# Four gate/up phases in a row, then four down phases, in a gated mix of linear attention and a GEGLU block

## The chip, the cores and the metric

The kernel runs on one core of a Trainium2 chip. The metric is device time in microseconds (us). Most executions of one kernel agree within some 0.3%, which is about 0.9 us here. Besides the timed runs each kernel has one profiled execution, whose trace gives the start of each instruction to the nanosecond. All timed runs used here are fast, with a granted TensorE clock of 1.00 (0.999 in some). Two kernels, `half` and `alloc`, were run only once, so that their state is unknown.

## The reference

```python
def reference(x, wqkv, w_phi, wo, w_gate, w_up, w_down, gate_w):   # S = 2048, D = 640, F = 1728
    g = sigmoid((x * gate_w).sum(-1, keepdims=True))
    a = linear_attention(x, wqkv, w_phi) @ wo     # 32 heads: num / den per head, then @ wo
    b = (gelu(x @ w_gate) * (x @ w_up)) @ w_down
    return g * a + (1 - g) * b
```

The 2048 tokens are four blocks of 512. "Gate/up phase b" (g0 to g3) computes the product `gelu(x @ w_gate) * (x @ w_up)` of block b, transposed, into a buffer `hT`. "Down phase b" (d0 to d3) multiplies it with `w_down` and adds the attention output `goT @ wo` in the same accumulators. The attention numerators, one for each of the 16 tiles of 128 tokens, are small matmuls with a chain of VectorE work behind them, which ends in a transposing DMA that writes `goT`. They are strewn into the phases: two into g1, the others into the down phases.

## The kernel before

A gate/up tile is ten matmuls over all 128 rows of the array, five for the gate and five for up (the code here and below is abridged; `# ...` marks some of the cuts):

```python
def gateup(self, b, c, banks):
    oldw, hT = (self.oldw, self.hT0) if b % 2 == 0 else (self.oldk, self.hT1)   # two buffers
    # ... c < 13:
    for w, wk, bk in ((self.wg_sb, "wg", banks[0]), (self.wu_sb, "wu", banks[1])):
        for kt in range(self.KD):                                  # KD = 5
            self.mm(bk, 0, 512, w[:, kt, c*P:(c+1)*P], xs(kt), kt == 0, kt == self.KD - 1, ...)
    # ACT: gl = gelu(bank 0);  DVE: hT[:, c, :] = bank 1 * gl
```

The down phase uses the array as two tiles of 64 rows each. Two matmuls run at once, one on the rows 0 to 63 and one on 64 to 127, each for another tile of tokens and into another bank:

```python
def down_pair(self, t0, banks, widths):
    def mm(r, j, h, c, opens, x, n):
        t, a = ts[j], 64 * r
        if c <= NFC:
            lhs, rhs = hT[a:a+64, c, tt*P:(tt+1)*P], self.wd_sb[a:a+64, c, w0:w0+w]      # product @ w_down
        else:
            lhs, rhs = self.goT[a:a+64, gs, k, :], self.wo_sb[a:a+64, k, w0:w0+w]        # attention @ wo
        sc.op("pe", ...)
    for q in range(2 * nw):
        h, opens = q % nw, q < nw
        cs = list(range(NFC + 1 if opens else NFC)) + [NFC + 1 + k for k in range(KD)]   # goT comes last
        for x, c in enumerate(cs):
            for r in (0, 1):
                mm(r, r if opens else 1 - r, h, c, opens, x, len(cs))
            # ... eviction after the last
            yield None
```

And the order of the phases:

```python
at = (1, 31, 61, 91)               # steps of a down phase at which a numerator is put in
gateups(0, state)
gateups(1, first_nums)             # numerators 0 and 1
for b in range(self.NB):
    downs(b, {at[k]: 4*b + 2 + k for k in range(4 if b < 3 else 2)})
    if b < 2:
        gateups(b + 2, none)       # so: g0 g1 d0 g2 d1 g3 d2 d3
```

The kernel orders everything by semaphores that its small scheduler sets from declared reads and writes.

The softmax here doesn't subtract the row's maximum and nothing guards it: scores larger than these inputs give would overflow.

## Time and profile before

| | before |
|---|---|
| median of 3 runs before the prediction | 289.03 us (288.50 to 289.33) |
| span of the profiled execution | 287.9 us |
| TensorE (PE) busy | 98% |
| start to start of matmuls in a gate/up phase | 216 ns |
| start to start of pairs of matmuls in a down phase | 132 or 133 ns to the next pair, 3 or 4 ns inside a pair |

From the page of the kernel before: the span, the line of the busiest engine (busy time, share, instructions) and the chain of work that ended last, by engine and by line (L351 is the helper that issues gate/up, L708 the down phase).

```profile
span 287.9 us, 7001 instructions
...
PE 282.0 (98%) x3017; PEld 185.7 (65%) x3032; DVE 174.8 (61%) x353; ACT 105.0 (36%) x199; POOL 5.3 (2%) x36
...
PE 96%; DMA 1%; ACT 1%; issue 1%; ACTq 0%
```

The chain is nearly all matmuls, so only what shortens or lengthens the sequence of TensorE counts. The table by stage (start and end; then length, busy time and number of instructions for PE, weight loads PEld, VectorE, ScalarE and GpSimd; clock; share and rate of DMA) shows a down phase and the gate/up phase behind it:

```profile
core 0: us, PE busy (x) PEld busy (x) DVE busy (x) ACT busy (x) POOL busy (x), PEclk, DMA share, GB/s
140.40:162.40 22.00, 21.84 (x378) 15.86 (x379) 16.15 (x45) 2.96 (x7) 0.00 (x0) 1.00 0.23 47
162.40:191.40 29.00, 28.89 (x134) 12.99 (x137) 9.15 (x14) 9.17 (x16) 0.00 (x0) 1.00 0.03 12
```

VectorE is busy for 16.15 of 22 us in a down phase, because of the numerators, and for a third of a gate/up phase. TensorE has no room in either. Two groups of the page, the gate matmuls and their weight loads (count; busy time and mean ns of one; idle time before):

```profile
L351 PE MATMUL ps<-xT,wg_sb 128*128 128x512 bf16 (+1 forms) x265 | 63.8, 379 | 0.6 <-issue 0.5
...
L351 PEld LDWEIGHTS ps<-xT,wg_sb 128*128 128x128 bf16 (+1 forms) x270 | 26.0, 99 | 29.1 <-issue 0.5
```

Each of these matmuls has a weight load of its own, but 265 stand against 270: matmul records can be missing from a trace.

The timeline at the switch from d0 to g2 (start, length, engine, instruction group; in brackets the idle time before and what ended it):

```profile
start us, us, engine line op out<-in xcount [idle before <-releaser]
161.64 0.57 PE L708 MATMUL ps<-wo_sb,goT 64*128 64x320 bf16 x6
162.37 1.03 PE L351 MATMUL ps<-xT,wg_sb 128*128 128x512 bf16 x4 [0.16 <-issue]
```

The weight loads of the same kernel at the same time:

```profile
162.14 0.76 PEld L351 LDWEIGHTS ps<-xT,wg_sb 128*128 128x128 bf16 x5 [0.26 <-issue]
```

The chain at the same place (start, length, what) puts the idle time of 0.16 us into it:

```profile
159.90 2.31 PE ps L708 x34
162.21 0.16 issue
162.37 1.67 PE ps L351 x7
```

The border of two down phases, d2 and d3, in the timeline, where nothing is switched:

```profile
263.40 0.84 PE L708 MATMUL ps<-wo_sb,goT 64*128 64x320 bf16 x10
...
264.08 0.30 PE L708 MATMUL ps<-wd_sb,hT 64*128 64x320 bf16 x2
...
264.97 0.36 DVE L667 RECIPROCAL RH<-ps 128x32 f32<-128x32 f32 x1 [4.08 <-PE ps L651]
```

Matmuls follow one another without an idle gap here, and VectorE had idled for 4.08 us before the first numerator of d3: the VectorE work of d2 was done in time.

### The profile page before, as it was taken

The page shows a single profiled execution, that of the slowest core. Times are in us where ns is not written, and L with a number is a line of the kernel's source. Part 1 is how long each engine was busy: PE and PEld are TensorE (multiplying, and loading weights), DVE is VectorE, ACT ScalarE, POOL GpSimd, SP SyncE. Part 2 cuts the span into 40 slices and gives each one's busy share as a digit, 9 for nine tenths or more (in the row PEclk, how much of TensorE's full clock was granted, in tenths as well). Part 3 has the DMA queues.
Part 4 walks back from the last instruction along what each step waited for, and adds up shares of the span by engine and source line. Part 5 has one row for each costly group of instructions (what it writes and reads, how often), then busy time and mean ns, then how long its engine had stood idle before and what let it go on. Part 6 is the DMA issues. An engine that isn't in the chain of part 4 may idle for free.

```text
span 287.9 us, 7001 instructions
## 1 busy us (share of the span) xinstructions
PE 282.0 (98%) x3017; PEld 185.7 (65%) x3032; DVE 174.8 (61%) x353; ACT 105.0 (36%) x199; POOL 5.3 (2%) x36
## 2 busy tenths in 40 slices
PE   7999999999999999999999999999999999999996
PEld 4566689999994444444577544457754445777785
DVE  2338999999977553568588142258823324883801
ACT  3357897687663322322111332211133231112111
POOL 7000000000000000000000000000000000000000
PEclk9999999999999999999999999999999999999999
DMA  7999996000002000011014200001330000132221
GB/s 232 191 166 240 368 367 204 0 2 2 2 0 48 0 0 0 3 24 23 2 25 86 78 0 0 0 3 25 57 96 11 0 0 2 25 45 78 67 72 48
DMA packets 36937, 18.67 MB, mean 65 GB/s; under 512 B 28970, under 2 KB 36394, under 8 KB 36906
## 3 DMA queue, kind: packets, MB, share of 16 engines
q1 hardware_dynamic: 36096, 17.86, 24.8%
q8 instruction: 24, 0.39, 0.6%
q10 hardware_dynamic: 810, 0.35, 0.5%
q14 instruction: 7, 0.06, 0.1%
HBM read 9.04 MB, written 2.62 MB: 40 GB/s over the span
## 4 chain that ended last, share of the span: by engine, by line
PE 96%; DMA 1%; ACT 1%; issue 1%; ACTq 0%
PE ps L351 60%; PE ps L708 28%; PE ps L651 2%; PE ps L363 2%; PE ps L449 2%; DMA xtok<-in_A_x_dram 1%; PE ps L331 1%; PE ps L290 1%; ACT Ek L413 0%; ACT Eq L518 0%; ACT outsb L721 0%; ACT gcol L416 0%; PE ps L313 0%; ACTq L42 0%
## 5 line engine op out<-in xcount | busy, mean ns | idle before, releaser
L625 DVE TENSOR_TENSOR hT<-ps,gl 128x512 bf16<-128x512 f32 x52 | 35.7, 690 | 65.1 <-PE ps L351 65.0
L708 PE MATMUL ps<-wd_sb,hT 64*128 64x320 bf16 (+2 forms) x918 | 66.2, 288 | 0.0
L351 PE MATMUL ps<-xT,wg_sb 128*128 128x512 bf16 (+1 forms) x265 | 63.8, 379 | 0.6 <-issue 0.5
L351 PE MATMUL ps<-xT,wu_sb 128*128 128x512 bf16 (+1 forms) x263 | 63.3, 379 | 0.5 <-issue 0.2
L623 ACT ACTIVATE gl<-ps 128x512 bf16<-128x512 f32 x52 | 30.9, 596 | 70.3 <-PE ps L351 66.0
L708 PEld LDWEIGHTS ps<-wd_sb,hT 64*128 64x128 bf16 x918 | 43.1, 94 | 15.6 <-ACT gl L623 0.8
L351 PEld LDWEIGHTS ps<-xT,wu_sb 128*128 128x128 bf16 (+1 forms) x270 | 26.5, 99 | 29.7 <-DVE hT L625 0.5
L351 PEld LDWEIGHTS ps<-xT,wg_sb 128*128 128x128 bf16 (+1 forms) x270 | 26.0, 99 | 29.1 <-issue 0.5
L721 ACT ACTIVATE outsb<-ps,Gm 128x320 bf16<-128x320 f32 (+2 forms) x31 | 14.5, 515 | 75.6 <-PE ps L708 75.6
L351 PE MATMUL ps<-w,xT 128*64 128x512 bf16 (+6 forms) x398 | 41.6, 325 | 0.2
L351 PEld LDWEIGHTS ps<-w,xT 128*64 128x64 bf16 (+1 forms) x400 | 35.8, 107 | 4.8
L708 PE MATMUL ps<-wo_sb,goT 64*128 64x320 bf16 (+2 forms) x340 | 27.8, 288 | 0.0
L351 PE MATMUL ps<-xT,wq 128*64 128x512 bf16 (+1 forms) x184 | 26.1, 380 | 0.4 <-ACT Eq L518 0.3
L433 DVE TENSOR_TENSOR Ek<-Ek,Dk 128x640 bf16<-128x640 bf16 x32 | 25.0, 822 | 0.6
L678 DVE TENSOR_TENSOR O<-ps,RH 128x640 bf16<-128x640 f32 x32 | 24.7, 814 | 0.0
L424 DVE TENSOR_REDUCE Dk<-Ek 128x64 f32<-128x1280 bf16 x16 | 23.7, 1479 | 0.1
L413 ACT ACTIVATE Ek<-ps 128x640 bf16<-128x640 f32 x32 | 20.7, 703 | 3.7 <-PE ps L351 3.7
L518 ACT ACTIVATE Eq<-ps 128x512 bf16<-128x512 f32 x40 | 21.7, 605 | 1.1 <-PE ps L351 0.8
L708 PEld LDWEIGHTS ps<-wo_sb,goT 64*128 64x128 bf16 x340 | 16.1, 94 | 5.4
L351 PEld LDWEIGHTS ps<-xT,wq 128*64 128x64 bf16 (+1 forms) x185 | 15.3, 108 | 3.4 <-ACT Eq L518 0.8
L405 ACT ACTIVATE vaug<-ps 128x640 bf16<-128x640 f32 x12 | 8.5, 706 | 12.1 <-PE ps L351 12.1
L667 DVE RECIPROCAL RH<-ps 128x32 f32<-128x32 f32 x16 | 5.7, 357 | 7.5 <-PE ps L651 6.8
(65 smaller groups left out, 148.0 us busy)
## 6 DMA issues: line engine op xcount, KB each, us to landing
out_dram<-outsb SPq DMA_DIRECT2D x7, 320.0 KB, 2.3
wd_sb<-in_B_w_down_dram SPq DMA_DIRECT2D x1, 2080.0 KB, 14.2
wg_sb<-in_B_w_gate_dram SPq DMA_DIRECT2D x1, 1120.0 KB, 5.8
wu_sb<-in_B_w_up_dram SPq DMA_DIRECT2D x1, 1120.0 KB, 8.3
wg_sb<-in_B_w_gate_dram SPq DMA_DIRECT2D x1, 960.0 KB, 9.6
wu_sb<-in_B_w_up_dram SPq DMA_DIRECT2D x1, 960.0 KB, 10.2
w<-in_A_wqkv_dram SPq DMA_DIRECT2D x5, 160.0 KB, 4.0
wo_sb<-in_A_wo_dram SPq DMA_DIRECT2D x1, 800.0 KB, 9.9
```

The source lines that it names most:

```text
L351: self.sc.op("pe", lambda e: e.matmul(self.ps[a:z, bank * 512 + c0:bank * 512 + c0 + n], lhs[:, a:z], rhs, start=first, stop=fin), reads=r ...
L363: sc.op("pe", lambda e, c0=c0, n=n, bk=bk, col=col: e.matmul(self.bank(bk)[:, col:col + n], self.xT[:, kt, t * P:(t + 1) * P], self.w3[:, ...
L405: self.sc.op("act", lambda e: e.activation(self.vaug[:, sv, :, 0:self.DH], self.bank(B, self.D).rearrange("p (h d) -> p h d", d=self.DH), ...
L413: self.sc.op("act", lambda e, s=s, scale=scale: e.activation(self.Ek[:, se, s, :], self.ps[:, o:o + self.D], AF.Exp, scale=scale), reads=[ ...
L424: sc.op("dve", lambda e: e.tensor_reduce(self.Dk[:, se, 0, :].rearrange("p (s h) -> p s h", h=H), self.Ek[:, se, :, :].rearrange("p s (h d ...
L433: sc.op("dve", lambda e, v=v, r=r: e.tensor_tensor(v, v, r, ALU.mult), reads=[("Rk", se)], writes=[("Ek", se, s)])
L518: sc.op("act", lambda e, s=s, scale=scale: e.activation(self.Eq[:, s, i, b * self.BT:(b + 1) * self.BT], self.bank(bank), AF.Exp, scale=sc ...
L623: sc.op("act", lambda e: e.activation(self.gl[:, slot, :], self.bank(banks[0]), AF.Gelu_apprx_tanh), reads=[("ps", banks[0])], writes=[("g ...
L625: sc.op("dve", lambda e: e.tensor_tensor(hT[:, c, :], self.bank(banks[1]), self.gl[:, slot, :], ALU.mult), reads=[("ps", banks[1]), ("gl", ...
L678: dve(lambda e, o=o, f=f, s=s: e.tensor_tensor(o, V[s][:, :, :, 0:DH], f, ALU.mult), rb + [key(6 + s)], [("O", s, sl)], guard=old)
L708: sc.op("pe", lambda e: e.matmul(self.bank(bk, w), lhs, rhs, start=opens and x == 0, stop=end and not opens, skip_group_check=True), reads ...
L721: sc.op("act", lambda e: e.activation(dst, self.bank(bk, w), AF.Copy, scale=g), reads=rd, writes=wr)
```

## The change

The new order is g0 g1 g2 g3 d0 d1 d2 d3. All four products must then live at once. A third buffer is allocated, and the fourth product is put over `x` of the first three blocks, which nobody reads any more after g2. Its core:

```diff
+        self.hT2 = T("hT2", [P, NFC, BT], BF16)
...
+    def hT(self, b, c):
+        if b == 3:
+            return self.xT[:, c // 3, (c % 3) * self.BT:(c % 3 + 1) * self.BT]
+        return (self.hT0, self.hT1, self.hT2)[b][:, c, :]
...
-        oldw, hT = (self.oldw, self.hT0) if b % 2 == 0 else (self.oldk, self.hT1)
-        hk = b % 2
+        old = (self.oldw, self.oldk, [], [("xT", t) for t in range(12)])[b]
+        hT, hk = self.hT(b, c), b
...
         gateups(1, first_nums)
+        gateups(2, none)
+        gateups(3, none)
         for b in range(self.NB):
             downs(b, {at[k]: 4 * b + 2 + k for k in range(4 if b < 3 else 2)})
-            if b < 2:
-                gateups(b + 2, none)
```

Not one matmul, eviction or transfer is saved. What goes away are switches between the two uses of the array: of three from gate/up to down one stays, and of two back none.

More of the change, by code (lines that the diff above doesn't have):

```diff
@@ L624, in gateup @@
                   reads=[("ps", banks[0])], writes=[("gl", slot)], guard=self.oldw)
-            sc.op("dve", lambda e: e.tensor_tensor(hT[:, c, :], self.bank(banks[1]), self.gl[:, slot, :], ALU.mult),
-                  reads=[("ps", banks[1]), ("gl", slot)], writes=[("hT", hk, c)], guard=oldw)
+            sc.op("dve", lambda e: e.tensor_tensor(hT, self.bank(banks[1]), self.gl[:, slot, :], ALU.mult),
+                  reads=[("ps", banks[1]), ("gl", slot)], writes=[("hT", hk, c)], guard=old)
         else:
@@ L636, in gateup @@
                 sc.op("dve", lambda e: e.tensor_tensor(
-                    odd(hT[64 * r:64 * r + 64, c, :]), odd(self.ps[64:128, bk * 512:bk * 512 + 512]),
+                    odd(hT[64 * r:64 * r + 64, :]), odd(self.ps[64:128, bk * 512:bk * 512 + 512]),
                     odd(self.gl[64:128, slot, :]), ALU.mult),
-                    reads=[("ps", bk), ("gl", slot)], writes=[("hT", hk, c, r)], guard=oldw)
+                    reads=[("ps", bk), ("gl", slot)], writes=[("hT", hk, c, r)], guard=old)
     def num(self, t):
@@ L691, in down_pair @@
         nw = len(widths)
-        hk = t0 // 4 % 2
-        hT = (self.hT0, self.hT1)[hk]
+        hk = t0 // 4
         last = t0 + 2 == self.NT
@@ L701, in mm @@
             if c <= NFC:
-                lhs, rhs = hT[a:a + 64, c, tt * P:(tt + 1) * P], self.wd_sb[a:a + 64, c, w0:w0 + w]
+                lhs, rhs = self.hT(hk, c)[a:a + 64, tt * P:(tt + 1) * P], self.wd_sb[a:a + 64, c, w0:w0 + w]
                 rd = [("hT", hk, c), "wd"] if c < NFC else [("hT", hk, 13, r), ("wd13", r)]
```

## The prediction

> **What bounds the kernel now.** TensorE. The page gives PE busy 282.0 us of a span of 287.9 us (98%); the chain of waits is 96% PE. From 86 us on, where the gate/up (g) and down (d) phases lie, no wait for another engine stands in the chain until the last eviction (0.37 us). The table by stage shows the granted clock at 1.00 everywhere. Down phases begin at 140.36, 191.38 and 242.40 us in the timeline, 51.02 us apart, of which 29.0 us is a gate/up phase (135 matmuls 216 ns apart) and 22.0 us a down phase.
>
> **What the change does.** Every matmul, eviction and transfer stays, in number and size; only the order of phases differs. Before: g0 g1 d0 g2 d1 g3 d2 d3. After: g0 g1 g2 g3 d0 d1 d2 d3. Two of the three g-to-d switches, and both d-to-g switches, disappear.
>
> The down phases and the attention numerators use the array as two tiles of 64 rows, the gate/up phases all 128 rows. The Trainium skill, "TensorEngine Tiling (Array Packing)", Key Properties, says that changing the tiling mode drains TensorE. The trace agrees and gives the size, in starts of successive matmuls: within g 216 ns, at the switch to d 311 ns (+95, three times); within d 132 ns from pair to pair, at the switch back 454 ns (+322, twice, of which the timeline shows 0.16 us as idle PE). Down to down (d2 to d3, at 264.08 us) shows no gap: d2 lasts 21.68 us from start to start, d0 with its switch back 22.01 us.
>
> Removed: 2 x 0.322 + 2 x 0.095 = 0.83 us, all on PE's chain.
>
> **What it could add, and why I expect nothing.**
> - The numerators now follow one another through 88 us of down work, without gate/up phases in which VectorE could catch up. But one takes VectorE 4.19 us (141.26 to 145.45), one is issued each 4.47 us, four in a phase, and then VectorE idles (4.08 us from d2 to d3). No backlog carries over.
> - goT for the next phase: the last numerator of d2 left VectorE at 260.9 us, plus 2.6 us to landing, and is wanted after 266 us. The same margin holds for d0/d1 and d1/d2.
> - The output buffers alternate; pairs of tiles are about 11 us apart and a store lands in 2.3 us.
> - The fourth product over x waits only for PE's matmuls of g2, done before by PE's order.
> - The third buffer needs no guard. Loads of w_down and w_out kept nobody waiting before.
> - VectorE's and ScalarE's work per gate/up tile (0.69 and 0.60 us) is far under 2.16 us of matmuls.
>
> **Predicted.** 289.03 - 0.83 = 288.2 us; eight times in ten between 287.5 and 288.9 us (the three runs before spread over 0.83 us, as much as the gain). Faster by over 2%: 0.01; within 2%: 0.98; slower by over 2%: 0.01.
>
> **What would show it right.** Matmul starts: gate/up phases with 216 ns across their borders, one +95 ns switch, none of +322 ns; down phases of 21.7 us from start to start; VectorE idle 4 us between the numerators of successive down phases; span near 287.1 us.
>
> **What would make it wrong.** A wait of a numerator's matmuls for VectorE, or of the output projection for goT, in d1 or d2; the product over x making matmuls that read x or load weights from it slower than 216 or 132 ns; moved buffer addresses changing other durations; or the clock falling in the long stretch of one kind of work.

## The result

| | before | changed |
|---|---|---|
| median of 6 runs | 288.97 us (288.30 to 289.33) | 288.37 us (287.87 to 289.37) |
| ratio of the fast runs | | 0.9986, 95% interval 0.9965 to 1.0007 |
| median of 6 more runs of the changed kernel (`again`; 11 of before) | 289.00 us | 288.68 us; ratio 0.9986, 0.9966 to 1.0007 |
| profiled span | 287.9 us | 286.9 us |

A ratio is the mean time of one kernel's fast runs over that of the other's in the same rounds, so it is not quite the ratio of the medians. 0.9986 of 289 us is a gain of 0.4 us. The interval holds a gain of 1.0 us (so also the 0.83 us predicted) and a loss of 0.2 us, so the clock alone doesn't tell whether the change helped; the trace does.

From the page of the changed kernel, the span, PE and the chain by engine:

```profile
span 286.9 us, 7006 instructions
...
PE 281.2 (98%) x3017; PEld 185.5 (65%) x3032; DVE 174.7 (61%) x353; ACT 105.0 (37%) x199; POOL 5.3 (2%) x36
...
PE 93%; SPq 3%; DMA 2%; ACT 1%; issue 1%; ACTq 0%
```

The chain by engine now contains waits for DMA and SPq (the issuing queue). They lie in the first 15 us, in the loads of x and the weights, which the change doesn't touch. Two stages of the changed kernel: the end of g1 with most of g2 (which starts at 139.6 us), and d0.

```profile
132.20:161.20 29.00, 28.88 (x133) 13.16 (x135) 11.27 (x18) 8.35 (x14) 0.00 (x0) 1.00 0.03 6
...
197.90:219.60 21.70, 21.70 (x377) 15.85 (x378) 16.07 (x45) 2.83 (x6) 0.00 (x0) 1.00 0.25 48
```

In the window of d0 PE is busy for all of 21.70 us, and from the start of d0 (197.93 us) to that of d1 (219.61 us) it takes 21.68 us, as d2 did before. The border of d0 and d1 looks like that of d2 and d3 did before; in the changed kernel's timeline:

```profile
218.93 0.84 PE L714 MATMUL ps<-wo_sb,goT 64*128 64x320 bf16 x10
...
219.61 0.30 PE L714 MATMUL ps<-wd_sb,hT 64*128 64x320 bf16 x2
...
220.49 0.36 DVE L674 RECIPROCAL RH<-ps 128x32 f32<-128x32 f32 x1 [4.07 <-PE ps L658]
```

And in its chain of work, where the line of idle time is gone (L658 is a numerator):

```profile
215.97 3.94 PE ps L714 x58
219.91 0.39 PE ps L658 x20
220.30 3.80 PE ps L714 x55
```

The numerator's first VectorE instruction again comes after 4.07 us of idle VectorE; no work piled up. TensorE waits for no `goT` anywhere in this trace.

**Where the microsecond of the span came from.** The two spans differ by 1.0 us, which looks like more than the 0.83 us predicted. It isn't. I cut each trace at the last of the short attention matmuls ahead of the long run of gate/up matmuls (three tiles of g0 lie earlier, among the attention work), and at the start of the last eviction:

| part | before | changed | difference |
|---|---|---|---|
| to the last short attention matmul | 85.89 us | 85.16 us | -0.73 |
| from there to the last eviction (all phases) | 199.40 us | 199.00 us | -0.40 |
| from there to the end of the span | 2.63 us | 2.78 us | +0.15 |

The first part is common code, and it is luck: over the eleven traces of this study it took anything from 85.16 to 86.19 us, and in a second profile of the changed kernel (`again`) it took 86.08 us. That second profile has a span of 287.7 us, but its middle part is again exactly 199.00 us. The middle part, which repeats within 0.01 us, is the measure to use from here on. The change is worth **0.40 us** in it, not 0.83 us.

### The profile page after: what moved, and what is told of

Its sections match the earlier page's. It is cut to its first block, busy times and chain, and to the rows that moved or that the text cites. A ratio compares the mean times of both kernels' runs of the same rounds, so it can differ in the third digit from the quotient of the medians.

```text
span 286.9 us, 7006 instructions
## 1 busy us (share of the span) xinstructions
PE 281.2 (98%) x3017; PEld 185.5 (65%) x3032; DVE 174.7 (61%) x353; ACT 105.0 (37%) x199; POOL 5.3 (2%) x36
## 4 chain that ended last, share of the span: by engine, by line
PE 93%; SPq 3%; DMA 2%; ACT 1%; issue 1%; ACTq 0%
PE ps L352 60%; PE ps L714 28%; PE ps L658 2%; DMA xT<-in_A_x_dram 2%; PE ps L450 2%; SPq L221 2%; PE ps L332 1%; SPq L234 1%; SPq L225 1%; ACT Ek L414 0%; ACT Eq L519 0%; SPq L217 0%; ACT outsb L727 0%; ACT gcol L417 0%; ACTq L42 0%
## 5 line engine op out<-in xcount | busy, mean ns | idle before, releaser
L352 PE MATMUL ps<-xT,wg_sb 128*128 128x512 bf16 (+1 forms) x265 | 63.8, 379 | 0.4 <-issue 0.2
L352 PE MATMUL ps<-xT,wu_sb 128*128 128x512 bf16 (+1 forms) x263 | 63.3, 379 | 0.5 <-DVE hT L632 0.2
L632 DVE TENSOR_TENSOR hT<-ps,gl 128x512 bf16<-128x512 f32 x39 | 26.7, 690 | 38.6 <-PE ps L352 38.5
L714 PE MATMUL ps<-wd_sb,hT 64*128 64x320 bf16 x648 | 49.5, 296 | 0.0
L352 PEld LDWEIGHTS ps<-xT,wu_sb 128*128 128x128 bf16 (+1 forms) x270 | 26.5, 99 | 29.8 <-DVE hT L632 0.5
L352 PEld LDWEIGHTS ps<-xT,wg_sb 128*128 128x128 bf16 (+1 forms) x270 | 26.2, 99 | 29.0 <-ACT gl L630 0.2
L352 PE MATMUL ps<-w,xT 128*64 128x512 bf16 (+6 forms) x398 | 41.6, 325 | 0.4 <-DMA xT<-in_A_x_dram 0.2
L352 PEld LDWEIGHTS ps<-w,xT 128*64 128x64 bf16 (+1 forms) x400 | 35.8, 107 | 5.1 <-DMA xT<-in_A_x_dram 0.4
L714 PEld LDWEIGHTS ps<-wd_sb,hT 64*128 64x128 bf16 x648 | 31.0, 94 | 12.1 <-issue 0.4
L352 PE MATMUL ps<-xT,wq 128*64 128x512 bf16 (+1 forms) x184 | 26.1, 381 | 0.4 <-ACT Eq L519 0.3
L632 DVE TENSOR_TENSOR xT<-ps,gl 128x512 bf16<-128x512 f32 x13 | 9.0, 691 | 18.2 <-PE ps L352 18.2
L352 PEld LDWEIGHTS ps<-xT,wq 128*64 128x64 bf16 (+1 forms) x185 | 15.3, 109 | 3.4 <-ACT Eq L519 0.8
L714 PE MATMUL ps<-wd_sb,xT 64*128 64x320 bf16 (+2 forms) x270 | 16.7, 269 | 0.0
```

The costliest lines, as they stand in the source:

```text
L352: self.sc.op("pe", lambda e: e.matmul(self.ps[a:z, bank * 512 + c0:bank * 512 + c0 + n], lhs[:, a:z], rhs, start=first, stop=fin), reads=r ...
L632: sc.op("dve", lambda e: e.tensor_tensor(hT, self.bank(banks[1]), self.gl[:, slot, :], ALU.mult), reads=[("ps", banks[1]), ("gl", slot)], ...
L714: sc.op("pe", lambda e: e.matmul(self.bank(bk, w), lhs, rhs, start=opens and x == 0, stop=end and not opens, skip_group_check=True), reads ...
```

## The experiments

The question left is why the removed switches were worth half of what I had read off the trace. Theory 1: the +322 ns for the way back was a misreading. The five weight loads beside four matmuls in the timeline before, and the 270 against 265 of the page, suggest that the record of the first matmul after each switch was missing. Then 454 ns is two steps, about 238 + 216, and the switch costs +106. Theory 2: the way back does cost +322 ns, and the new order lost 0.4 us somewhere else, for example in numerators that press on VectorE or in the product placed over x.

### Many switches: sw128 and sw64

To multiply the suspected cost, extra matmuls are put behind 26 tiles of g2 and g3 of the changed kernel, into accumulator banks that are free there. Their result is thrown away, so the outputs stay right. `sw128` uses the array as the gate/up phase does and is the control; `sw64` differs only in using two 64-row tiles.

```diff
+        def extra(idx):
+            if idx == 13:
+                return
+            for r in (0, 1):                                 # sw128: for r in (0,)
+                sc.op("pe", lambda e: e.matmul(
+                    self.ps[0:128, (2 + 2*r)*512:(2 + 2*r)*512 + 320],
+                    self.wd_sb[64*r:64*r + 64, 0, 0:128],    # sw128: rows 0:128
+                    self.wo_sb[64*r:64*r + 64, 0, 0:320],    # sw128: rows 0:128
+                    start=True, stop=True, skip_group_check=True),
+                    reads=["wd", "wo"], writes=[("ps", 2 + 2*r)], signal=False)
-        gateups(2, none)
-        gateups(3, none)
+        gateups(2, extra)
+        gateups(3, extra)
```

> The changed kernel, with one extra 128-row matmul (N=320) after each of 26 gate/up tiles of the third and fourth gate/up phases, into banks that are free there: no change of tiling, the control for sw64. All theories: 26 x about 0.136 us = 3.5 us over the changed kernel, so about 291.9 us; starts of successive matmuls 136 and 216 ns, no longer gap at the inserts.

> The same 26 inserts as two concurrent 64-row matmuls (N=320), so 26 added switches into the 64-row tiling and 26 back. Theory 1 (the record of the first matmul after each switch back is missing in the profile of before, a switch back costs +106 ns and not +322): 26 x (0.095+0.106) = 5.2 us over sw128, about 297.1 us, and a gap of about 238 ns after most inserts, with 454 ns only where a record is missing. Theory 2 (the switch back costs +322 ns as the prediction read it): 26 x 0.417 = 10.8 us over sw128, about 302.7 us, and 454 ns after nearly all.

Measured: `sw128` 292.14 us, `sw64` 297.52 us (4 runs each; before 288.83 us; ratios 1.012 and 1.0305; one run of the kernel before, of 410 us, is left out of the ratios). The difference is 5.38 us. Theory 1 had said 5.2 and theory 2 had said 10.8. An insert of `sw64` in the timeline (L802 is the insert, L352 gate/up):

```profile
143.58 0.81 PE L352 MATMUL ps<-xT,wu_sb 128*128 128x512 bf16 x3
144.32 0.31 PE L802 MATMUL ps<-wo_sb,wd_sb 64*128 64x320 bf16 x2
144.57 0.60 PE L352 MATMUL ps<-xT,wgu_sb 128*128 128x512 bf16 x2
```

And the distances between the starts of matmuls, worked out from the starts of all records:

```
                                      sw64, 26 inserts     sw128, 26 inserts
gate/up -> insert                     311 or 312 ns        215 or 216 ns
insert (last of it) -> gate/up        238 or 239 ns        135 or 136 ns
next step inside gate/up              226 or 227 ns        216 ns
every other step inside gate/up       215.8 ns (mean)      215.8 ns (mean)
```

All 26 ways back show 238 or 239 ns, none 454. A switch into the 64-row tiling costs 311.6 - 215.8 = 96 ns; a switch back costs 238.3 - 132.5 = 106 ns and 10.9 ns more in the step after it. Together that is 0.21 us for a pair of switches. Theory 2 is out.

The kernel before had held the answer too, and I overlooked it: each of the two numerators in g1 switches into the 64-row tiling and back, with all records there. The way in is 311 or 312 ns; the way back is 134 ns, where the steps between a numerator's own pairs are 36 ns, and 226 ns for the step after it. That is about 98 + 10 ns for a way back, not 322.

### The same switches, but with real work: split and half

`split` has all buffers of the change, but cuts d0 and d1 in two and puts halves of g2 and g3 between: four pairs of switches more than the changed kernel. `half` does half of the change: one pair more than the changed kernel and one fewer than before.

```diff
 split:
+        for b in (0, 1):
+            downs(b, nums(b), (0,));  gateups(b + 2, none, slice(0, 7))
+            downs(b, nums(b), (2,));  gateups(b + 2, none, slice(7, 14))
+        for b in (2, 3):
+            downs(b, nums(b))
 half:
         gateups(2, none)
-        gateups(3, none)
         for b in range(self.NB):
+            if b == 2:
+                gateups(3, none)
```

> The changed kernel's buffers and all its work, in the order g0 g1, first half of d0, half of g2, second half of d0, half of g2, the same for d1 with g3, then d2 d3: four switches to the 64-row tiling and four back more than the changed kernel. From the first gate/up matmul to the last eviction (199.05 us before, 198.64 after) theory 1 expects 198.64 + 4 x 0.20 = 199.4 us, theory 2 198.64 + 4 x 0.417 = 200.3 us; the timed difference is at the edge of what three rounds resolve. If leaving VectorE without gate/up phases to catch up cost anything in the changed kernel, split would lose less than 4 x 0.20 us.

> Half of the change: g0 g1 g2 d0 d1 g3 d2 d3, one switch pair fewer than before and one more than in the changed kernel. From the first gate/up matmul to the last eviction theory 1 expects 199.04 - 0.21 = 198.83 us, theory 2 198.62; no wait of TensorE for goT.

The expectations speak of the first gate/up matmul as the starting point. That choice has the very flaw under study: its record is missing in some traces (the first recorded one then stands 357 ns behind the attention matmul) and present in others (130 ns). I therefore compare from the last attention matmul, as in the table above.

| kernel | pairs of switches against the changed kernel | last attention matmul to last eviction | difference |
|---|---|---|---|
| changed, twice | 0 | 199.00 and 199.00 us | |
| half | +1 | 199.19 us | +0.19 |
| before | +2 | 199.40 us | +0.40 |
| split | +4 | 199.83 us | +0.83 |

A straight line of 0.19 to 0.21 us per pair, in real work. It leaves nothing for theory 2 to lose elsewhere: `split` gives VectorE its gate/up phases back and isn't a bit cheaper than the switches account for. Timed, `split` is at 289.40 us and 1.0023 of before (1.0003 to 1.0043); 0.42 us more than before, which the line demands, would be 1.0015. `half` had a single run, of unknown state (289.31 us), and I use its trace only.

In the trace of `split` all four records behind the ways back are there. The kind of switch that I had misread, here in the middle of d0, in the timeline of `split`:

```profile
150.19 0.84 PE L714 MATMUL ps<-wo_sb,goT 64*128 64x320 bf16 x10
150.97 1.25 PE L352 MATMUL ps<-xT,wg_sb 128*128 128x512 bf16 x5
```

And its weight loads:

```profile
150.97 0.76 PEld L352 LDWEIGHTS ps<-xT,wg_sb 128*128 128x128 bf16 x5 [0.26 <-issue]
```

Five gate matmuls, no idle time. The starts at the way back are 228 ns and then 226 ns apart, which sum to 454: exactly the one step seen in the kernel before. The weight loads show where the lost record belongs. In `split` the first two loads start at 150.965 and 150.980 us and the first matmul at 150.969, 4 ns after the first load. The kernel before has the same two loads, at 162.136 and 162.151 us, so its first matmul started at about 162.140, which is 228 ns after the last one of d0 (161.912).

### Addresses: alloc

> The kernel before with only the third buffer allocated, unused, so that everything after it has the changed kernel's addresses. If addresses matter, the 199.04 us from the first gate/up matmul to the last eviction move, or the 85.5 us to it are the changed kernel's; otherwise 199.04 us, and a start between 85.3 and 86.3 us.

```diff
         self.BD = T("BD", [P, KD, 8 * DH], BF16)
+        self.hT2 = T("hT2", [P, NFC, BT], BF16)       # the kernel before, buffer unused
```

The middle part took 199.41 us against 199.40, so moving the buffers made no difference here. One run, 289.29 us, of unknown state. The first part took 85.91 us.

### What makes up the price of a switch: sw32

> As sw64, with weights of 32 columns instead of 128. If the price of a switch is the weight load of the new tiling laid bare (94 ns for 128 columns), the entry gets cheaper by most of 94 ns and the way back does not: about 26 x 0.07 = 1.8 us under sw64. If it is a drain of the array of fixed length, the time is that of sw64 within 0.5 us.

```diff
-                    self.ps[0:128, ...], self.wd_sb[64*r:64*r + 64, 0, 0:128],
+                    self.ps[0:32, ...],  self.wd_sb[64*r:64*r + 64, 0, 0:32],
```

Measured 297.33 us; the switch into the tiling took 309 to 310 ns instead of 311 to 312, the way back 238 to 240. At first sight that speaks for a drain of fixed length. But look at the inserted instructions (count; shortest, median and longest duration in ns; first and last start; form), first of `sw64`:

```profile
L802 PEld LDWEIGHTS ps<-wo_sb,wd_sb x52: 92/92/93, 141.8 to 204.5; 64*128 64x128 bf16 x52
L802 PE MATMUL ps<-wo_sb,wd_sb x52: 306/306/307, 141.8 to 204.5; 64*128 64x320 bf16 x52
```

The same of `sw32`:

```profile
L802 PEld LDWEIGHTS ps<-wo_sb,wd_sb x52: 88/88/89, 142.6 to 205.2; 64*32 64x32 bf16 x52
L802 PE MATMUL ps<-wo_sb,wd_sb x52: 306/306/307, 142.6 to 205.2; 64*32 64x320 bf16 x52
```

A weight load of 32 columns lasts 88 ns by the trace, one of 128 columns 92. So the experiment hardly changed what it was to change. (Nor is the recorded duration the pace of loading: inside a numerator, loads of 128 columns start every 39 ns in each of the two tiles.)

The traces do show that at a switch no load is hidden. In the control `sw128` each inserted matmul and each first matmul after it has its load started 214 or 134 ns ahead, right behind the start of the matmul before. In `sw64` all 78 of these loads (three for each insert) start only 4 or 5 ns ahead of their matmuls; the loads of the inserts, in the timeline:

```profile
144.32 0.10 PEld L802 LDWEIGHTS ps<-wo_sb,wd_sb 64*128 64x128 bf16 x2 [0.42 <-issue]
```

Whether the price is this exposed load, or a drain that also holds the load back, stays open. What is settled is the size of the price, and that loads of fewer columns lowered it by only about 3 ns.

### A wait that the inserts uncovered: early128 and early

The sum of `sw128` didn't close at first: 199.00 + 26 x 0.1358 (the steps above) = 202.53 us, but the middle part took 203.88. The kernels before and after show no wait of TensorE for `goT`; this one does. In the timeline, TensorE stops within the second pair of tiles of d0, at a use of `goT`:

```profile
215.05 0.30 PE L714 MATMUL ps<-wo_sb,goT 64*128 64x320 bf16 x1
216.43 0.58 PE L714 MATMUL ps<-wo_sb,goT 64*128 64x320 bf16 x5 [1.08 <-DMA goT<-Og]
```

The chain of `sw128` runs through the DMA there:

```profile
211.91 4.48 DMA goT<-Og
...
216.43 0.48 PE ps L714 x5
```

This transposing DMA took 4.48 us to land, while 2.57 us is usual. Two things came together.

The first is thin slack. From the records I worked out, for each pair of tiles, the time from the landing of the second tile's `goT` to its first use: 0.89 us for tile 3 in the kernel before and 0.55 us in the changed one, 0.95 and 0.93 us for tile 7, 0.94 us in both for tile 11, and 0.18 and 0.16 us for the last tile. The order of the phases hardly touches these, because the numerator of tile 4b+3 is started and used within the same down phase. It does cut those of tiles 5 and 9 from 32 us to 2.8 us.

The second is what delays the landing. The DMA engines also carry the fetches of instructions, which the page counts as a queue of their own (packets, MB, share of the engines' time):

```profile
q8 instruction: 24, 0.39, 0.6%
```

In the eleven traces there are 176 such transposes. In 68 of them a 16 KB fetch began within 2.3 us of the issue: they landed after 3.86 us in the median, and all but one after 2.76 to 5.22 us. Of the other 108, 106 landed after 2.56 to 2.66 us, two later. Stores of the output don't explain it: one was in flight during 14 of the 68 transposes and during 39 of the 108, and 38 of those 39 landed within 2.65 us. The fetches come about once for 253 recorded instructions of TensorE (24 for 6084 in the kernel before), so which transpose meets one should depend on how many instructions have gone before, and each kernel has its own pattern. In the kernel before and in the changed one, the fetches meet the transposes of even tiles, which have time to spare. The inserts moved them onto odd ones: tile 3 in `sw128` (1.33 us after TensorE wanted it), tile 11 in `sw64` (0.82), tiles 7 and 11 in `sw32` (0.89 together). The delay less the changed kernel's slack gives these losses: 4.48 - 2.57 - 0.55 = 1.36 us for `sw128`, 4.33 - 2.57 - 0.94 = 0.82 us for `sw64`.

That fetches delay the transposes is a very regular coincidence rather than an experiment of its own. To test that thin slack turned the delay into lost time, `early128` starts each numerator one place earlier.

```diff
-            if idx in (4, 8):
+            if idx in (4, 8, 12):                  # three numerators in g1
...
-            downs(b, {at[k]: 4 * b + 2 + k for k in range(4 if b < 3 else 2)})
+            downs(b, {at[k]: 4 * b + 3 + k for k in range(4 if b < 3 else 1)})
```

> sw128 with every attention numerator one place earlier (three instead of two in the second gate/up phase), which gives each transposed goT 4.47 us more before its first use. In sw128 one goT overlapped a fetch of instructions, landed after 4.48 us instead of 2.57, and TensorE stood 1.08 us. If that thin slack (0.9 us when a landing takes 2.57 us) was the cause: no wait for goT, the down phases 86.2 us minus the moved numerator instead of 87.6, and one more switch pair (+0.21 us): about 0.9 us less than sw128, 291.3 us. If the wait had another cause: 292.3 us.

> The changed kernel with every attention numerator one place earlier, as in early128 but without inserts. In the changed kernel no transposed goT was late, so more slack can win nothing, and the third numerator in the second gate/up phase adds one switch pair: from the last short attention matmul before the first gate/up tile to the last eviction 199.00 + 0.21 = 199.21 us, time within 0.3 us of the changed kernel. If thin slack did cost the changed kernel something that the chain does not show, this span is below 199.0 us.

`early128` took 291.83 us (`sw128`: 292.14 in another batch; ratios to before 1.0103 and 1.012). The timed gain is smaller than expected and within the noise. In the trace no wait for `goT` is left. But the fetches moved too: tile 3 now landed after 2.60 us, and the transpose that needed 5.22 us was that of tile 12, an even one. So this run alone doesn't show that the added slack was what helped. The middle part fell from 203.88 to 202.72 us: -1.33 for the late landing that is gone, +0.21 for the third numerator in g1, which is one more pair of switches, would be 202.76. TensorE at the same place in the timeline of `early128`, without a wait:

```profile
215.80 0.57 PE L714 MATMUL ps<-wo_sb,goT 64*128 64x320 bf16 x6
```

`early` is the same on the changed kernel: 288.75 us and 0.9995 of before (0.9964 to 1.0025), middle part 199.19 us where 199.21 was expected. Here the slack itself was tested: the last tile's transpose landed after 4.12 us, 1.55 us late, and TensorE did not wait; `goT` still lay ready for 2.74 us. The 0.16 us of the changed kernel would not have covered that. So thin slack cost the changed kernel nothing in its traces, and guarding against it costs 0.2 us. I had no version that beats the changed kernel.

**The books.** With 199.00 us for the changed kernel, 0.1358 us for an insert, 0.2125 us for each pair of switches around an insert (0.2092 in `sw32`, from 309.0, 238.4 and 225.9 ns) and the late landings:

| kernel | sum | measured middle part |
|---|---|---|
| sw128 | 199.00 + 26 x 0.1358 + 1.33 = 203.86 | 203.88 us |
| sw64 | 199.00 + 26 x (0.1358 + 0.2125) + 0.82 = 208.88 | 208.90 us |
| sw32 | 199.00 + 26 x (0.1358 + 0.2092) + 0.89 = 208.86 | 208.86 us |
| early128 | 199.00 + 26 x 0.1358 + 0.21 = 202.74 | 202.72 us |

## Why the prediction was right or wrong

- **The time.** Predicted 288.2 us, range 287.5 to 288.9; measured 288.37 and, in a second batch, 288.68 us. Both lie in the range, and "within 2%" was right. But that is luck more than insight: the range is as wide as the noise, and the total would have been in it with half the gain, as it in fact was.
- **"Within g 216 ns, at the switch to d 311 ns (+95)".** Right: 311 or 312 ns at every such switch of all kernels.
- **"Within d 132 ns from pair to pair, at the switch back 454 ns (+322)".** This step failed. The 454 ns span a matmul whose record is missing; the true steps are 228 and 226 ns, an excess of 0.11 us. The 0.16 us "idle PE" in the chain before is the same artefact. The switch back was the right thing to remove, but its cost was taken three times too large. So the term "2 x 0.322 + 2 x 0.095 = 0.83 us" should have been 2 x 0.107 + 2 x 0.096 = 0.41 us; measured 0.40 us. The hint stood in the same timeline: five weight loads beside four matmuls.
- **"d2 lasts 21.68 us from start to start, d0 with its switch back 22.01 us".** This comparison, which seemed to confirm +322, took the start of g2 from the same incomplete records, and so repeats the error instead of checking it. A check that works is the period of 51.02 us, whose ends are both recorded: 135 x 0.2158 = 29.13 us for a gate/up phase and 21.68 us for a down phase leave 0.21 us for the pair of switches.
- **Nothing added.** Right: VectorE idles 4.07 us at the border of d0 and d1, TensorE waits for nothing in the new down phases, matmuls that read or load from x keep their 215.8 and 132 ns, the clock stays at 1.00.
- **"goT for the next phase ... the same margin holds".** Right as far as it goes (2.8 us), but I had named the wrong margin as the one to watch. Those inside a phase are 0.55 to 0.95 us, and 0.16 us at the end. They held in these traces because the instruction fetches fell on transposes of even tiles; I hadn't looked at the fetches.
- **"Span near 287.1 us".** Measured 286.9 us, right for a wrong reason: 0.73 us of the drop came from the first 86 us, and the next profile of the same kernel had 287.7 us.

## What to carry to other kernels

Before you price a gap between two instructions from a trace, count the instructions on both sides of it against the program (weight loads are a good second witness), because one missing record looks exactly like a stall; and multiply a suspected small cost until the clock can see it, with a control that differs in nothing else. Compare traces over a stretch whose ends are always recorded and which leaves the loads at the start out: here it repeats to 0.01 us where whole runs scatter by 1 us. Regrouping phases to avoid changes of the array's tiling was safe but small here, 0.2 us per pair of switches, and transfers with under 1 us between their usual landing and their use, which cost nothing in the changed kernel, cost 0.8 to 1.3 us once extra matmuls stood ahead of them.

## What the Trainium skill lacked or had wrong

- "TensorEngine Tiling (Array Packing)", Key Properties, says that changing the tiling mode drains TensorE, without a size. The traces agree that a switch costs time, though they don't show whether it is a drain, and give the size: +96 ns from 128-row to 64-row tiles and +106 to 117 ns back (the latter over two steps), 0.21 us for both; 5.5 us for 26 pairs.
- "TensorE: Matmul & The Clock Gate", LDWEIGHTS (loading the stationary operand), gives a weight load about (columns / 1.2) ns and so would let 32 columns load in 27 ns and 128 in 107 ns (estimates from that page). The recorded durations in these traces are 88 ns for 32 columns and 92 ns for 128, in 64-row tiles, while loads of 128 columns follow one another every 39 ns in one tile of a numerator; the price of a pair of switches fell by only 3 ns with the narrow load.
- "Runtime: NRT & Kernel Launch", Instruction fetch mechanics, says that each engine's sequencer drives a DMA queue of its own which refills 16 KiB blocks, and that the cost is mostly hidden. The traces show such fetches as 16384-byte packets (8192 bytes on a second queue), and no wait of TensorE put down to them directly; what the page lacks is that data transfers may be held up: transposing DMAs that met one landed after 2.8 to 5.2 us instead of 2.57 us (68 and 108 cases), and TensorE then stood up to 1.08 us.
- No page that I read warns that single matmul records can be absent at the same place in several traces: behind the way back from a down phase in the kernel before, in `half` and in `alloc` (454 or 455 ns), but never in the 56 such places of `sw64`, `sw32` and `split` (228 to 240 ns). In the kernel before the loss is regular: inside the gate/up phases a step of 431 or 432 ns, twice the usual 216, comes back about every 10.8 us, or 50 matmuls.
